# Loading the second x tile from ScalarE's queue in a fused layernorm, attention and gated-MLP kernel

## The chip, the cores and the metric

The kernel runs on one core of a Trainium2 chip. The metric is device time in microseconds (us) of one execution; a value for a kernel is the median over several executions. The profile is one execution recorded by the hardware profiler. Its span, from the first to the last instruction, is a little shorter than the device time of the same execution.

## The reference

All matrices are bf16. x has 2048 rows of 640 values.

```
xn = layernorm(x)                          # over the 640 values of a row
q, k, v = xn @ wqkv                        # 32 heads of 20
logits: each row against rows s, s-2, ..., s-14 (8 of them), masked at the start
o = softmax(logits) * v, summed over the 8
return x + (o reshaped) @ wo + ((xn @ w_gate) * (xn @ w_up)) @ w_down
```

## The kernel before

The rows of x are cut into 16 tiles of 128. A tile is loaded with its rows on the 128 partitions (buffer XST), normalised into XNS, transposed so that its 640 columns lie on the partitions in five chunks (XNT), and multiplied with the weights. The first tiles are transposed by TensorE (L434), later ones by DMA.

The order of work is written out by hand. Every operation is recorded in program order with what it reads and writes; a small scheduler gives each engine its operations in that order, with semaphore waits where data cross engines. So each engine, and each engine's queue of DMA issues, works strictly in the order of the code. Nearly all loads are issued by one helper, so they all carry line 294 in the profile: on SyncE's queue (SPq), or on ScalarE's (ACTq) where the code says so.

The start of the program is what matters here:

- L297 to L307: constants. ScalarE's first instruction is a tiny square root (L324), which brings the load of its function table with it.
- L325: tile 0 is loaded in two halves, one by SyncE and one by ScalarE.
- L328: tile 1 is loaded; L329: the five chunks of the weights of q, called w0 to w4 here (each 128 rows of 640 values, 160 KB as a tile of x is); then tiles 2 and 3, the chunks for k, tiles 4 to 7, and so on.

```
    for half, eng in ((0, "sp"), (1, "act")):
        dst = XST[:, 0, half * DHALF:(half + 1) * DHALF]
        dma(dst, xhbm[0:TS, half * DHALF:(half + 1) * DHALF], w=[dst], name=f"xh{half}", eng=eng)
    x_load(1)
    for c in range(NCH):
        wqkv_load(0, c)
    x_load(2)
    x_load(3)
```

Tile 0's mean and variance are taken by VectorE (L372, L378, L384), its square root by ScalarE (L385), its reciprocal and the normalising by VectorE (L404, L419). Tile 1's sums are taken by ScalarE in the meantime: one pass for the mean (L392), one for the variance (L394), then the square root (L397); VectorE follows with L404 and L419, in two parts of 256 and 384 columns. On ScalarE these three stand behind the square root of tile 0.

TensorE runs matmuls on zeros first (L453), then the five transposes of tile 0 (L434), then the product of tile 0 with w0 to w4, five matmuls of 128 columns for each chunk (L492). Tile 1's five transposes stand between the matmuls with w3 and those with w4; the copies of the transposes out of PSUM are VectorE's (L445) and ScalarE's (L447). Then come tile 1's matmuls (L492), the product for k with two tiles at once (L773), and the rest of the kernel: projections (L499, L475), the gated MLP (L638), its down projection with the attention's output projection (L665, L697). While these run, VectorE does the attention (from L522 on).

Of the kernel before, what the change touches and what calls it, by code (L numbers as in the profile page):

```python
# [211 lines left out]
def build_kernel(nc, A_x, A_wqkv, A_wo, B_x, B_w_gate, B_w_up, B_w_down, out):  # L212
# [80 lines left out]
    def dma(o, i, r=(), w=(), name="", eng="sp", group=None):  # L293
        return op(eng, lambda e: e.dma_start(o, i), r=r, w=w, dma=True, name=name, group=group)  # L294
# [15 lines left out]
    def x_load(t, eng="sp"):  # L310
        dma(XST[:, t % NXS, :], xhbm[t * TS:(t + 1) * TS, :], w=[XST[:, t % NXS, :]], name=f"xld{t}", eng=eng)
# [13 lines left out]
    for half, eng in ((0, "sp"), (1, "act")):  # L325
        dst = XST[:, 0, half * DHALF:(half + 1) * DHALF]
        dma(dst, xhbm[0:TS, half * DHALF:(half + 1) * DHALF], w=[dst], name=f"xh{half}", eng=eng)
    x_load(1)  # L328
    for c in range(NCH):  # L329
        wqkv_load(0, c)  # L330
    x_load(2)
# [622 lines left out]
def bass_parallel_sum__sliding_local_dilated__glu_gated_bilinear__prompt_kernel(  # L954
    nc, A_x, A_wqkv, A_wo, B_x, B_w_gate, B_w_up, B_w_down, out
):
    build_kernel(nc, A_x, A_wqkv, A_wo, B_x, B_w_gate, B_w_up, B_w_down, out)
# [28 lines left out]
```

## Time and profile before

| what | value |
|---|---|
| median of 4 runs | 252.62 us (252.4 to 253.11) |
| profiled execution, device time | 252.48 us |
| its span | 251.1 us |
| TensorE busy | 247.0 us, 98% of the span |
| VectorE busy | 215.7 us, 86% |
| ScalarE busy | 114.0 us, 45% |

Times in the profile count from the start of the span. PE is TensorE, DVE VectorE, ACT ScalarE, SP SyncE; SPq and ACTq are DMA issues on those engines' queues. The duration of an issue is the time that the issuing engine's sequencer takes, not the transfer; the time from issue to landing is given apart. Matmuls are pipelined, so one takes longer (about 0.22 us) than the distance from its start to the next one's. In the table of DMA queues q1 is the row that SyncE's loads run on, q10 the row of ScalarE's.

### The profile page before, as it was taken

Reading aid. Unit: us, or ns where it says so; the run is one execution under the profiler, and the core shown is the slowest. Engines: PE = TensorE matmul, PEld = TensorE weight load, DVE = VectorE, ACT = ScalarE, POOL = GpSimd, SP = SyncE. Lnnn points to the kernel's source line nnn. Section 1 sums busy time; section 2 is a strip of 40 time slices with the busy share of each in tenths; the row PEclk is TensorE's granted clock in tenths of the full one; section 3 lists DMA queues with packets and bytes.
Section 4 is the critical chain, followed back from the end, with each engine's and each line's share of the span. In section 5 each row is a group of like instructions: output and inputs, shape, how many; then the busy total and the mean of one; then the engine's idle time right before and its main releaser. Section 6 shows DMA issues by size and latency. Waiting matters only on the chain.

```text
span 251.1 us, 3245 instructions
## 1 busy us (share of the span) xinstructions
PE 247.0 (98%) x1274; PEld 128.9 (51%) x1294; DVE 215.7 (86%) x255; ACT 114.0 (45%) x203; POOL 32.6 (13%) x41
## 2 busy tenths in 40 slices
PE   8999999999999999999999999999999999999997
PEld 3995555555544444444444444444444444445775
DVE  4879999999999953999999994899999999996212
ACT  5476657555555557555555553225555111011000
POOL 1000001043345231002231100002000000200200
DMA  6999869854787472355369962197500011490561
GB/s 194 300 260 198 106 140 409 235 114 76 146 146 136 87 135 42 130 206 104 64 125 263 402 211 42 39 333 63 90 0 3 21 30 32 67 124 21 81 153 52
DMA packets 33775, 33.78 MB, mean 134 GB/s; under 512 B 17984, under 2 KB 30272, under 8 KB 33728
## 3 DMA queue, kind: packets, MB, share of 16 engines
q1 hardware_dynamic: 27280, 24.13, 35.0%
q0 software_dynamic: 6192, 9.31, 22.7%
q8 instruction: 10, 0.16, 0.3%
q10 hardware_dynamic: 288, 0.13, 0.2%
q14 instruction: 5, 0.04, 0.0%
HBM read 14.42 MB, written 4.59 MB: 76 GB/s over the span
## 4 chain that ended last, share of the span: by engine, by line
PE 96%; DMA 1%; SPq 1%; issue 1%; DVE 0%
PE PS L638 41%; PE PS L665 22%; PE PS L475 21%; PE PS L697 7%; PE PS L499 2%; DMA WQKV<-in_A_wqkv_dram 1%; PE PS L773 1%; PE PS L492 1%; SPq L294 1%; PE PS L434 0%; DVE FOUT L701 0%
## 5 line engine op out<-in xcount | busy, mean ns | idle before, releaser
L638 PE MATMUL PS<-XNT,WU 128*128 128x512 bf16 x237 | 59.0, 379 | 0.2
L638 PE MATMUL PS<-XNT,WG 128*128 128x512 bf16 x232 | 57.9, 379 | 0.4
L475 PE MATMUL PS<-XNT,WQKV 128*128 128x512 bf16 x245 | 53.7, 379 | 0.3
L605 DVE TENSOR_TENSOR PVB<-VO,ATB 128x10240 f16<-128x10240 bf16 x8 | 43.9, 5490 | 0.2
L475 PEld LDWEIGHTS PS<-XNT,WQKV 128*128 128x128 bf16 x250 | 29.4, 118 | 24.4
L640 ACT ACTIVATE USX<-PS 128x512 bf16<-128x512 f32 x48 | 28.7, 597 | 22.6 <-PE PS L638 22.6
L638 PEld LDWEIGHTS PS<-XNT,WU 128*128 128x128 bf16 x240 | 23.5, 98 | 28.3
L638 PEld LDWEIGHTS PS<-XNT,WG 128*128 128x128 bf16 x240 | 23.5, 98 | 28.3
L600 DVE TENSOR_TENSOR PVB<-PVB 128x5120 f16<-128x5120 f16 (+1 forms) x16 | 34.5, 2156 | 0.3
L533 POOL DMA_DIRECT2D LOG<-PE x24 | 21.5, 910 | 59.8 <-DMA LOG<-PE 59.6
L640 ACT ACTIVATE HT<-PS 128x512 bf16<-128x512 f32 x36 | 21.5, 597 | 16.4 <-PE PS L638 16.4
L671 ACT ACTIVATE DT<-PS 128x512 f16<-128x512 f32 x15 | 8.9, 596 | 42.8 <-PE PS L665 39.7
L665 PE MATMUL PS<-HT,WD 128*128 128x512 bf16 x118 | 27.4, 379 | 0.1
L522 DVE TENSOR_TENSOR TMP<-QH,KH 128x2048 f16<-128x2048 bf16 x16 | 19.2, 1218 | 0.5 <-ACT KH L482 0.5
L665 PEld LDWEIGHTS PS<-HT,WD 128*128 128x128 bf16 x120 | 11.8, 98 | 14.1
L522 DVE TENSOR_TENSOR PP<-QH,KH 128x2048 f16<-128x2048 bf16 x16 | 18.9, 1218 | 0.0
L527 DVE TENSOR_TENSOR PP<-PP,TMP 128x4096 f16<-128x4096 f16 x8 | 18.3, 2291 | 0.2
L665 PE MATMUL PS<-VO,WO 128*128 128x512 bf16 x74 | 18.4, 379 | 0.0
L701 DVE TENSOR_TENSOR FOUT<-PS,XR 128x320 bf16<-128x320 f32 (+2 forms) x9 | 4.1, 455 | 15.5 <-PE PS L697 15.5
L533 POOL DMA_DIRECT2D PE<-PP x8 | 8.4, 1045 | 61.5 <-DVE PP L528 61.5
L643 DVE TENSOR_TENSOR HT<-HT,USX 128x512 bf16<-128x512 bf16 x36 | 14.3, 417 | 1.7 <-ACT USX L640 1.7
L482 ACT ACTIVATE VO<-PS 128x512 bf16<-128x512 f32 x20 | 11.8, 593 | 7.2 <-PE PS L475 7.2
(71 smaller groups left out, 220.8 us busy)
## 6 DMA issues: line engine op xcount, KB each, us to landing
PE<-PP POOLq DMA_DIRECT2D x8, 512.0 KB, 5.0
ATB<-LOG SPq DMA_DIRECT2D x8, 512.0 KB, 4.9
LOG<-PE POOLq DMA_DIRECT2D x24, 128.0 KB, 2.7
WG<-in_B_w_gate_dram SPq DMA_DIRECT2D x1, 1920.0 KB, 8.1
WU<-in_B_w_up_dram SPq DMA_DIRECT2D x1, 1920.0 KB, 14.8
WD<-in_B_w_down_dram SPq DMA_DIRECT2D x1, 1920.0 KB, 10.1
out_dram<-in_A_x_dram SPq DMA_DIRECT2D x1, 1920.0 KB, 10.2
out_dram<-FACC POOLq DMA_DIRECT2D x3, 640.0 KB, 6.6
```

What stands on the lines that cost most here:

```text
L475: op("pe", (lambda l, x, c: lambda e: e.matmul(PS[:, b, :], l, x, start=(c == 0), stop=(c == NCH - 1)))(l, x, c), r=[l, x], w=[PS[:, b, :] ...
L482: op("act", lambda e: e.activation(o, PS[:, b, :], ACT.Copy, scale=sc), r=[PS[:, b, :]], w=[o], name=f"pev{which}_{m}_{j}")
L522: return (1.22, lambda: op("dve", lambda e: e.tensor_tensor(o, qw, kw, ALU.mult), r=[q, k], w=[o], name=f"prod{h}_{p}_{c}"))
L527: (2.3, lambda: op("dve", lambda e: e.tensor_tensor(a, a, b, ALU.add), r=[a, b], w=[a], name=f"psum{h}_{p}")),
L533: op("pool", lambda e: e.dma_start(o, i, accum_op=ALU.add), r=[o, i], w=[o], dma=True, name=name)
L600: return lambda: op("dve", lambda e: e.tensor_tensor(o, x, y, ALU.add), r=[x, y], w=[o], name=f"{name}_{b}")
L605: lambda: op("dve", lambda e: e.tensor_tensor(PVB[:], vw, aw, ALU.mult), r=[v, a], w=[PVB[:]], name=f"pv_{b}")),
L638: op("pe", (lambda l, x, c: lambda e: e.matmul(PS[:, b, :], l, x, start=(c == 0), stop=(c == NCH - 1)))(l, x, c), r=[l, x], w=[PS[:, b, :] ...
L640: op("act", lambda e: e.activation(o, PS[:, b, :], ACT.Copy), r=[PS[:, b, :]], w=[o], name=f"guev{which}_{m}_{j}")
L643: h_pending.append(lambda: op("dve", lambda e: e.tensor_tensor(h, h, o, ALU.mult), r=[h, o], w=[h], name=f"h{m}_{j}"))
L665: op("pe", (lambda l, x, i: lambda e: e.matmul(PS[:, b, :], l, x, start=(i == 0), stop=(i == n - 1)))(l, x, i), r=[l, x], w=[PS[:, b, :]], ...
L697: op("pe", (lambda l, x, i, b, wid: lambda e: e.matmul(PS[:, b, 0:wid], l, x, start=(i == 0), stop=(i == n - 1)))(l, x, i, b, wid), r=[l, ...
```

## The change

The load of x tile 1 gets ScalarE's queue in place of SyncE's. On ScalarE it stands behind the tiny square root with its table load and behind ScalarE's half of tile 0. On SyncE the weight chunks follow directly on its half of tile 0. No other operation, buffer or order is touched.

```diff
     for half, eng in ((0, "sp"), (1, "act")):
         dst = XST[:, 0, half * DHALF:(half + 1) * DHALF]
         dma(dst, xhbm[0:TS, half * DHALF:(half + 1) * DHALF], w=[dst], name=f"xh{half}", eng=eng)
-    x_load(1)
+    x_load(1, "act")
     for c in range(NCH):
         wqkv_load(0, c)
     x_load(2)
```

## Prediction, before the change was run

> **What bounds the kernel now.** First the page: the engine row and the chain that ended last.
>
> ```profile
> span 251.1 us, 3245 instructions
> PE 247.0 (98%) x1274; PEld 128.9 (51%) x1294; DVE 215.7 (86%) x255; ACT 114.0 (45%) x203; POOL 32.6 (13%) x41
> PE 96%; DMA 1%; SPq 1%; issue 1%; DVE 0%
> ```
>
> TensorE carries 96% of the chain, so a change in the loads can only matter where the other 4% lie. The chain in order of time (start, duration, what) shows that they lie in the first 7 us:
>
> ```profile
> 2.60 0.44 SPq L294
> 3.08 3.68 DMA WQKV<-in_A_wqkv_dram
> 6.76 0.14 issue
> 6.90 0.45 PE PS L492 x5
> 7.34 0.29 PE PS L434 x5
> ```
>
> SyncE issues its loads one after another, some 0.47 us apart: half of x tile 0, x tile 1, weight chunks w0 to w4. TensorE then waits for w3, issued at 3.08 and landed at 6.76. After 6.90 the chain is TensorE's own until VectorE's last add (0.29 us), with nothing between but issue gaps of 0.05 us, so **a shift of TensorE at about 7.3 us is a shift of the end, one for one**. Read next what surrounds 7.3, in the timeline (start, duration, engine, line):
>
> ```profile
> 0.75 1.28 ACT L324 ACT_TABLE_LOAD   x1 [0.75 <-PEq L971]
> 1.00 0.37 ACTq L294 DMA_DIRECT2D XST<-in_A_x_dram  x1
> ...
> 4.07 0.29 ACT L385 ACTIVATE SD<-MV,EPSC 128x1 f32<-128x1 f32 x1 [1.83 <-DVE MV L384]
> 4.27 0.72 ACT L392 ACTIVATE XNS<-XST 128x640 bf16<-128x640 bf16 x1
> ...
> 6.07 0.29 ACT L397 ACTIVATE SD<-MV,EPSC 128x1 f32<-128x1 f32 x1
> 6.40 0.16 DVE L404 RECIPROCAL SD<-SD 128x1 f32<-128x1 f32 x1 [0.29 <-ACT SD L397]
> 6.60 0.64 DVE L419 TENSOR_SCALAR XNS<-XST,MV,SD 128x256 bf16<-128x256 bf16 x2
> ...
> 7.18 0.45 PE L434 MATMUL PS<-IDENT,XNS 128*128 128x128 bf16 x5
> ```
>
> This is the second chain of tile 1: ScalarE sums it (L392, L394) from 4.27 on, its root comes at 6.07, VectorE normalises it in two parts (ends 6.95 and 7.24), TensorE transposes it from 7.18. Five transposes take 0.28 us or so of the chain, 0.056 each, so the third, the first that needs the second part, is due at about 7.29, some 0.05 us after that part is written. The chain of waits names w3; tile 1's chain is **as late as w3, within 0.05 us**.
>
> Last, how full the transfer engines are. Of the stretches of half a microsecond:
>
> ```profile
> 2.50:3.00 0.50, 0.50 (x2) 0.15 (x1) 0.09 (x1) 0.00 (x0) 0.00 (x0) 1.00 0.98 310
> 3.00:3.50 0.50, 0.50 (x2) 0.15 (x1) 0.50 (x2) 0.00 (x0) 0.00 (x0) 1.00 0.93 292
> ```
>
> The last two columns are DMA share and GB/s. From 2.0 to 6.5 us the share is 0.86 or more. The loads are drained, not issued, at the pace that counts.
>
> **What the Trainium skill says.** "DMA: Bandwidth & Descriptors", section "Issuing engines are not separate DMA queues": loads started by ScalarE and SyncE run on the same 16 engines and interleave; another issuer saves issue time only. Its section "Queues, rings and completion order" says that each DMA engine takes turns between the queues with work, packet by packet. The trace agrees as far as it goes: tile 0's two halves came on two queues and landed 2.1 us after issue each. "ScalarE: Activation LUTs", section "What ACT_TABLE_LOAD costs": 1283 ns; the trace has 1.28. "Perfetto Trace Analysis", section "Sequencer Loop": the sequencer pushes engine work into a queue and goes on. The trace agrees: the load on ACTq started at 1.00, while the table load ran to 2.03.
>
> **The change part by part.**
>
> *SyncE.* One issue (L294) leaves its queue. w0 starts at about 1.19 instead of 1.65, and w1 to w4, x2, x3 and the rest follow 0.46 us earlier. Cost or gain at the transfer engines: nearly none, since the same data (tile 0, tile 1, w0 to w3, six tiles of 160 KB) must still pass before w3 is complete, and the engines have been full since 2.0. At most the tenth that they stand empty from 3.5 to 5.5 us is filled: 0.2 us. And if w3 does land earlier, TensorE does its five matmuls earlier and stops at the transposes of tile 1, whose second part is not written before 7.24. So at most 0.05 us reaches the end. I take 0. The cover is tile 1's chain; without it the gain would be 0.2.
>
> *ScalarE's queue.* It gains one issue, right behind its half of tile 0: start 1.00 + 0.37 + 0.05 = 1.42, against 1.19 on SyncE. Nothing is queued behind it that is due before 4.07, so its 0.4 us costs ScalarE nothing. That the table load holds it up, I exclude for the likeliest case, as the first load was not held up. The two issuers also overlapped (SPq 0.74 to 1.13, ACTq 1.00 to 1.37) without a longer issue on either side.
>
> *Tile 1's transfer.* This is the part with a price. Count packets in the queue table asked from a given time to the end. q1 is SyncE's row, q10 ScalarE's, and a transfer of 128 rows has 144 packets: q10 has 288 for its two (half of tile 0, and a store at the end).
>
> ```profile
> q10 hardware_dynamic: 284, 0.13, 0.2%
> ...
> q10 hardware_dynamic: 144, 0.05, 0.1%
> ...
> q1 hardware_dynamic: 27011, 23.90, 35.0%
> ...
> q1 hardware_dynamic: 26857, 23.73, 34.9%
> ```
>
> From 2.2 on q10 has 284 left, from 2.8 on 144: the half of tile 0 began just before 2.2, 1.2 us after its issue, and was drained by about 2.65 (8 packets were left at 2.6). q1 had 27280 in all; 27011 are left at 3.0 and 26857 at 3.6, which is 154 in 0.6 us or **257 a microsecond** for one queue alone. Tile 1 before (288 packets into q1) was thus drained at about 3.08, and landed at 1.19 + 2.3 = 3.49.
>
> Afterwards tile 1's data can come at 1.42 + 1.2 = 2.62, and begins behind its own queue's half tile at 2.65. From then on w0 and w1 wait in SyncE's queue too, 0.46 us earlier than before, so the two queues take turns: 128 packets a microsecond for tile 1, 144 / 128 = 1.12 us, **drained at 3.78 instead of 3.08**.
>
> From mean drain to landing the slowest engine has to finish. That lag was 0.41 for tile 1, 0.59 for w0 (1.65 + 2.6 = 4.25, drained at about 3.66) and 1.2 for w1 (landed about 5.5, drained at 4.33). Tile 1 now is mixed with just these. Both ends: 0.41 gives 4.19, 1.2 gives 4.98. I take the middle, 0.8: **landing at 4.58**, and 0.04 to start (VectorE's first L372 began at 2.91, its half having landed near 2.85), so 4.62.
>
> *What waits.* L392 was ready at 4.27, after the root of tile 0; x1 had then 0.78 us to spare. Now L392 starts at 4.62: **0.35 late**; from both ends, 0 and 0.75. Behind it on ScalarE stand L394, the root L397 and the copy of tile 1's transposes (L447), all late alike; VectorE's L404 and L419 wait for the root, the transposes for L419, and w4's five matmuls and tile 1's thirty stand behind the transposes on TensorE. The 0.05 us of slack is within the rounding. VectorE's statistics of tiles 2 and 3 come after its copy of tile 1 and shift with TensorE, so no new wait opens there.
>
> *Sum.* 0 for SyncE, 0 for ScalarE's issue, +0.35 for tile 1: the profiled execution, span 251.1 and time 252.48, becomes 252.83. The median of the runs is 252.62, 0.14 above the profiled one; 252.62 + 0.35 is 252.97, say 253.0.
>
> **The rivals.** What a measurement of this kernel can tell from no change is about 0.2%, 0.5 us; the four runs span 0.7.
>
> - *Late by sharing*, the forecast: +0.1 to +0.8. For it: full transfer engines and a chain with 0.05 us of slack. Chance 0.55, about half of it (0.28) above 0.5, which is the side of a landing after 4.73.
> - *Hidden anyway*: tile 1 lands by 4.23, since the first engines to be free favour it or the lag stays at 0.41. Then 0, 252.6. For it: 0.78 us of spare before L392. Against: half the drain rate eats 0.70 of that before any lag. Chance 0.22.
> - *Held up on ScalarE*: the second load of a queue does wait for the table load or for the small ACTIVATE behind it (ends 2.24). Then data from about 3.45, 1.12 to drain, 0.8 lag: 5.4, L392 1.1 late, time 253.7, slower by 0.4%. It decides as soon as the issue starts later than about 1.57, since then the landing passes 4.73. Against: the issue at 1.00 under the table load. Chance 0.14. It is also the case in which the change is "behind the table load" in fact; in the forecast it isn't.
> - *Weights earlier*: w3 lands up to 0.4 us earlier and tile 1 in time. -0.05 for the cap at 7.24; if the cap is softer than I read it, -0.2, 252.4. Beyond -0.5 there is nothing to take: TensorE's whole stop between w2's and w3's matmuls is 6.47 (15 matmuls of 0.056 from 5.64) to 6.90, 0.43. Chance 0.09; 0.03 for faster by over 0.2%, chance of measurement included.
>
> **How the numbers follow.** Slower by over 0.2%: 0.28 + 0.14 = 0.42. Faster: 0.03. Within: 0.27 + 0.22 + 0.06 = 0.55. The time is that of the likeliest, 253.0. The range takes in the landing at its late end and most of the held-up case (253.7 and a little noise), and below the hidden case and half of the last: 252.4 to 253.8.
>
> **What would show it.** Right: on ACTq two issues, the second at about 1.4; SyncE's w0 at about 1.2; tile 1 from issue to landing some 3.2 us instead of 2.3; L392 at about 4.6 with an idle stretch ahead of it put down to DMA XST; the root L397 near 6.4 and the five transposes near 7.5. Wrong: L392 still at 4.27 (hidden); an issue on ACTq after 2.0 (held up); transposes before 7.1 (the cap isn't one); or a shift at 7.5 us that is not found again at the end.

## The result and the profile after

The changed kernel takes 253.01 us (median of 35 runs, 252.58 to 253.65) against 252.54 us for the kernel before in the same comparison (53 runs). The ratio is 1.0018, interval 1.0013 to 1.0023: **slower by 0.47 us**, 0.18%. The forecast was 0.35 us slower. The profiled execution took 252.74 us, its span is 251.4.

The timeline of the kernel after, in the stretch shown for the kernel before (start, duration, engine, line):

```profile
0.74 1.28 ACT L324 ACT_TABLE_LOAD   x1 [0.74 <-PEq L971]
1.00 0.85 ACTq L294 DMA_DIRECT2D XST<-in_A_x_dram  x2
...
1.19 2.31 SPq L294 DMA_DIRECT2D WQKV<-in_A_wqkv_dram  x5
...
4.14 0.29 ACT L385 ACTIVATE SD<-MV,EPSC 128x1 f32<-128x1 f32 x1 [1.91 <-DVE MV L384]
...
4.68 0.74 ACT L392 ACTIVATE XNS<-XST 128x640 bf16<-128x640 bf16 x1 [0.25 <-DMA XST<-in_A_x_dram]
...
6.50 0.29 ACT L397 ACTIVATE SD<-MV,EPSC 128x1 f32<-128x1 f32 x1
...
6.83 0.16 DVE L404 RECIPROCAL SD<-SD 128x1 f32<-128x1 f32 x1 [0.65 <-ACT SD L397]
...
7.03 0.64 DVE L419 TENSOR_SCALAR XNS<-XST,MV,SD 128x256 bf16<-128x256 bf16 x2
...
7.43 0.63 PE L434 MATMUL PS<-IDENT,XNS 128*128 128x128 bf16 x5 [0.17 <-DVE XNS L419]
```

Read it from the top. ScalarE's queue issues twice in a row from 1.00 to 1.85 (the second issue begins at 1.40), under the table load. The weights start at 1.19. ScalarE's sum of tile 1 (L392) starts at 4.68 instead of 4.27, and the bracket now names what ended the idle time before it: the transfer of XST. The root, the normalising and the transposes follow, 0.25 to 0.43 us later than before.

The table of TensorE's waits has changed its entry too. Before it was L492 waiting 0.2 us for w3:

```profile
PE PS L453 <- DVE EPSC L298: 1.0, 1, 1.0
PE PS L434 <- DVE XNS L419: 0.7, 2, 0.6
```

The wait for the weights is gone, and tile 1's transposes wait instead. (0.6 of the 0.7 belong to tile 0's transposes at 5.04, after the matmuls on zeros.) The two events that had met within 0.05 us have come apart: w3 comes a little earlier, and tile 1 later by more than that.

How much of this reaches the end? First the kernel before, then the changed one:

```profile
7.47 1.96 PE L492 MATMUL PS<-XNT,WQKV 128*128 128x128 bf16 x30
9.27 1.36 PE L773 MATMUL PS<-XNT,WQKV 128*128 128x256 bf16 x11
...
7.90 1.84 PE L492 MATMUL PS<-XNT,WQKV 128*128 128x128 bf16 x30
9.57 1.36 PE L773 MATMUL PS<-XNT,WQKV 128*128 128x256 bf16 x11
```

Tile 1's matmuls (L492) start 0.43 later. The product for k (L773) starts 0.30 later: the thirty matmuls took 1.84 us instead of 1.96, which caught up 0.12. From there the two traces run 0.30 apart to the end, which is the difference of the spans. It is less than the 0.47 of the medians, since the profiled execution was one of the quicker ones of the changed kernel (252.74, median 253.01).

One view misleads. The chain that ended last now shows other shares than before:

```profile
PE 92%; SPq 3%; DMA 3%; issue 1%; DVE 1%; ACT 0%
```

Followed in order of time, it leaves TensorE at 18.54 and goes to a load of x issued at 9.30. TensorE didn't stop there: the table of its waits has no such entry, and the gap there is 0.06 us, against 0.05 in the kernel before. An instruction that happened to end just then was taken for the releaser. The table of waits decides.

### The profile page after: what moved, and what is told of

It reads as the page before. It is cut to its first block, busy times and chain, and to the rows that moved or that the text cites. A ratio compares the mean times of both kernels' runs of the same rounds, so it can differ in the third digit from the quotient of the medians.

```text
span 251.4 us, 3245 instructions
## 1 busy us (share of the span) xinstructions
PE 246.7 (98%) x1274; PEld 128.7 (51%) x1294; DVE 216.0 (86%) x255; ACT 114.6 (46%) x203; POOL 32.6 (13%) x41
## 4 chain that ended last, share of the span: by engine, by line
PE 92%; SPq 3%; DMA 3%; issue 1%; DVE 1%; ACT 0%
PE PS L638 41%; PE PS L665 22%; PE PS L475 21%; PE PS L697 7%; SPq L294 3%; DMA XST<-in_A_x_dram 3%; DVE STATS L372 0%; DVE STATS L378 0%; ACT SD L385 0%; DVE FOUT L701 0%; DVE MV L384 0%; DVE SD L404 0%
```

## The experiments

Landings below are the last of a load's 16 engines in the trace. "Over before" is against the kernel before on the same chip. Where an edit adds a line, the profile's line numbers are higher by one or two.

**1. Tile 1 on SyncE's queue, behind w0 or behind w1.**

```diff
-    x_load(1)
     for c in range(NCH):
         wqkv_load(0, c)
+        if c == 0:        # in the second kernel: c == 1
+            x_load(1)
```

> Tile 1 stays on SyncE's queue, but behind w0. It is issued at about 1.65, later than in the changed kernel (1.42). Sharing theory (tile 1 lands late because its packets take turns with the weights'): alone in one queue it is drained behind w0 and lands at 4.2 to 4.3, where w0 landed before; L392 at 4.27 to 4.35; 0 to 0.15 us over the kernel before, about 0.35 faster than the changed one. Rival, the later issue as such costs: another 0.23 us later than in the changed kernel, 0.6 to 0.7 over before.

> Tile 1 on SyncE's queue behind w0 and w1, issued at about 2.12. A dose of lateness without a second queue. Sharing theory, with the end moving one for one: lands where w1 landed before, 5.0 to 5.6, L392 as late, 0.7 to 1.3 us over before. Rival, the start-up has slack that takes most of a delay in: under 0.5 over before.

Behind w0: 252.77 against 252.55, ratio 1.0009 (1.0001 to 1.0017), 0.22 over before. Behind w1: 253.85, ratio 1.0048 (1.0035 to 1.0061), 1.30 over before. Behind w0 the profiled execution had tile 1 landing at 4.69, later than I expected, but the median lies under the changed kernel's although the issue is later (1.65 against 1.40). The rival had 0.6 to 0.7 over before, so the later issue as such isn't the cause. The landing is as late as in the changed kernel, with one queue alone: here w0's packets stand ahead of tile 1's. Behind w1 the landing was 5.83, and ScalarE and TensorE followed it:

```profile
5.85 0.74 ACT L393 ACTIVATE XNS<-XST 128x640 bf16<-128x640 bf16 x1 [1.46 <-DMA XST<-in_A_x_dram]
...
8.60 0.57 PE L435 MATMUL PS<-IDENT,XNS 128*128 128x128 bf16 x4 [1.35 <-DVE XNS L420]
```

In this execution L392 (here L393) starts 1.58 later than in the kernel before, the transposes 1.42 later, and the span is 1.46 longer (252.61 against 251.15). The start-up takes in 0.12 of a delay of 1.58.

**2. A filler in tile 1's old place on SyncE's queue.** To give tile 1 on ScalarE's queue the engines alone for a while, SyncE issues a load that nobody reads before w0.

```diff
     x_load(1, "act")
+    dma(XR[:, 0, 0:16], xhbm[0:TS, 0:16], w=[XR[:, 0, 0:16]], name="fill")
     for c in range(NCH):
```

> The changed kernel, with a load of 4 KB that nobody reads in tile 1's old place on SyncE's queue, so that w0 to w4 go out at their times of before (about 1.65 and on). Only the queue of tile 1 differs from before. Sharing theory: w0's packets come 0.46 later, tile 1 has the engines alone at first and lands at 4.2 to 4.4; L392 at 4.3 to 4.4, 0 to 0.15 us over before. Rival, ScalarE's queue costs by itself (its issue, or a lower share for its row): lands near 4.6 as in the changed kernel, 0.4 to 0.5 over before.

252.99 against 252.55, ratio 1.0016 (1.0009 to 1.0022): 0.44 over before, as the rival had it. The profiled execution, with tile 1 at 4.08, was the fastest of its 21 runs (252.54): it shows what can happen, not what mostly does. The 4 KB filler adds 128 packets ahead of the weights, so I repeated it with one row of 32 bytes, and with two.

> As the run with the filler, but the filler is one row of 32 bytes on one partition, so that it takes SyncE's time and next to nothing of the transfer engines. Sharing theory: tile 1 lands at 4.0 to 4.3, w3 where it did in the kernel before (6.7 to 6.9), 0 to 0.2 us over before; what the filler run had above that came of its 128 small packets ahead of the weights. Rival, ScalarE's queue costs by itself: 0.35 to 0.5 over before again.

> Two such rows ahead of w0, so that w0 goes out 0.9 us later than in the changed kernel and tile 1 has the engines nearly alone. Sharing theory: tile 1 lands at 3.5 to 3.9 from the same issue at 1.42 that brought it to 4.66 beside w0; the end is then w3's, issued 0.47 later than in the kernel before: landing 6.8 to 7.2, 0 to 0.4 us over before. Rival, ScalarE's queue or its issue is what is slow: tile 1 at 4.0 or later.

One row: 253.06 against 252.63, ratio 1.0016 (1.0008 to 1.0025); tile 1 landed at 5.05. Two rows: 252.86, ratio 1.0004 (0.9996 to 1.0012); tile 1 at 4.64. A row takes 0.3 us of issue and not 0.47, so w0 went out at 1.55 and 1.81. Tile 1 missed the expectation in both.

**3. The same without fillers: SyncE waits before w0.** The load of w0 is recorded as reading a constant that GpSimd writes.

```diff
     def wqkv_load(g, c=None, eng="sp"):
         ...
-        dma(dst, wqkv_src[:, cs, g * D:(g + 1) * D], w=[dst], ...)
+        r = [IDENT[:]] if (g, c) == (0, 0) else []     # MSK0 in the second kernel
+        dma(dst, wqkv_src[:, cs, g * D:(g + 1) * D], r=r, w=[dst], ...)
```

> The changed kernel, with SyncE held before w0 by a wait for GpSimd's IDENT (ready at about 1.56) and no filler: w0 goes out at about 1.6, as in the kernel before, and nothing else is added to the transfer engines. Sharing theory: tile 1 has 0.4 us more of the engines alone and lands at 4.0 to 4.3, 0 to 0.2 us over before. Rival, tile 1 on ScalarE's queue is late whenever the weights start (its own packets are slow there, which the filler runs suggest): 4.5 to 5.0, 0.35 to 0.5 over before.

> The same with a wait for GpSimd's MSK0 (ready at about 1.85): w0 at about 1.9. Sharing theory: tile 1 lands at 3.6 to 4.0 and costs nothing; w3, issued 0.25 later than in the kernel before, lands at 6.8 to 7.1 and costs 0 to 0.3 us. Rival, slow in itself: tile 1 at 4.5 or later, 0.35 to 0.6 over before.

Wait for IDENT (w0 issued at 1.59): 253.02 against 252.56, ratio 1.0016 (1.0007 to 1.0024), tile 1 at 5.03. Wait for MSK0 (w0 at 1.88): 252.82, ratio 1.0006 (0.9997 to 1.0014), tile 1 at 4.91. So the landings are the rival's: **with w0 held back by 0.36 to 0.69 us, tile 1 still landed at 4.64 to 5.05 in four of five traces** (4.08 in the fifth). Where w0 was held back by 0.36 to 0.46, no time came back (0.43 to 0.46 over before). Where it was 0.62 and 0.69, about half did (0.23 and 0.26), at the edge of the noise, and that is inside what sharing had for these two. The queue table of the kernel with the wait for IDENT, asked from 2.6 and from 3.2 us to the end, shows that turn-taking can't be what held tile 1 up in that kernel:

```profile
q1 hardware_dynamic: 26992, 23.89, 33.9%
q10 hardware_dynamic: 294, 0.21, 0.4%
...
q1 hardware_dynamic: 26991, 23.88, 34.0%
q10 hardware_dynamic: 242, 0.15, 0.2%
```

In 0.6 us one packet passed on SyncE's row and 52 on ScalarE's, 87 a microsecond. In the kernel before, the same 0.6 us (q1 27120 at 2.6, 26962 at 3.2) passed 158 on one row, 263 a microsecond. The stretches of 0.4 us, with DMA share and GB/s in the last two columns, first of the kernel before:

```profile
2.80:3.20 0.40, 0.40 (x3) 0.12 (x2) 0.29 (x1) 0.00 (x0) 0.00 (x0) 1.00 0.99 314
```

and of the kernel with the wait:

```profile
2.40:2.80 0.40, 0.40 (x3) 0.12 (x2) 0.00 (x0) 0.00 (x0) 0.00 (x0) 1.00 1.10 171
2.80:3.20 0.40, 0.40 (x3) 0.13 (x2) 0.32 (x1) 0.00 (x0) 0.00 (x0) 1.00 0.84 90
```

The engines count as busy (0.84) but move 90 GB/s: each packet takes long. Tile 1 has them to itself and is slow.

Is this ScalarE's queue, and did it slow tile 1 in the changed kernel too? The queue table of a stretch gives the packets that passed in it and the share of the 16 engines' time that they took. Four stretches of 0.6 us: the wait for IDENT from 2.6, the changed kernel from 3.2 (both rows), and SyncE's row in the kernel with the 4 KB filler from 4.4:

```profile
q10 hardware_dynamic: 52, 0.06, 89.5%
...
q10 hardware_dynamic: 98, 0.11, 54.2%
q1 hardware_dynamic: 70, 0.08, 43.6%
...
q1 hardware_dynamic: 47, 0.05, 71.6%
```

Share times 0.6 us times 16, over the packets, is the mean time of one: 165 ns on ScalarE's row in the kernel with the wait, but **53 ns there in the changed kernel, beside 60 on SyncE's**, and 146 on SyncE's row in the last. So slow packets aren't confined to ScalarE's row, and they aren't what made tile 1 drain late in the changed kernel. The kernels that held w0 back had a slow spell of their own just as tile 1 began (85 to 169 ns a packet from 2.6 to 3.2, in all five), which undid what they were built to test. Why it came, these runs don't settle.

**4. ScalarE's loads ahead of the square root.** The square root with its table load moves behind the loads, once in the changed kernel and once in the kernel before (where ScalarE has only tile 0's half).

```diff
-    op("act", lambda e: e.activation(DUM[:, 0:1], EPSC[:, 0:1], ACT.Sqrt), ..., name="sqrt_preload")
     for half, eng in ((0, "sp"), (1, "act")):
         ...
     x_load(1, "act")
+    op("act", lambda e: e.activation(DUM[:, 0:1], EPSC[:, 0:1], ACT.Sqrt), ..., name="sqrt_preload")
```

> The changed kernel, with ScalarE's two loads ahead of the tiny square root. Sharing theory: issues at about 0.74 and 1.15, tile 1 0.2 to 0.27 earlier in the queue, landing at 4.35 to 4.5; 0.1 to 0.3 us over before. Rival, the square root and its table load hold the second load up: taking them away brings tile 1 to 3.6 or earlier and the whole loss goes.

> The kernel before with ScalarE's load of tile 0's half ahead of the tiny square root: the partner of the run in which the changed kernel got this and lost its whole 0.47 us. Sharing theory (there it was tile 1's earlier issue and landing): the kernel before has nothing to gain by it, -0.15 to +0.15 us. Rival, what came back there was tile 0's earlier half or the later table load: the kernel before gains 0.25 us or more as well.

On the changed kernel: 252.56 against 252.55, ratio 1.0001 (0.9993 to 1.0010), the loss is gone. On the kernel before: 252.55 against 252.63, ratio 0.9997 (0.9990 to 1.0003), no difference. The first, in the timeline:

```profile
0.74 0.89 ACTq L294 DMA_DIRECT2D XST<-in_A_x_dram  x2
...
1.67 1.28 ACT L328 ACT_TABLE_LOAD   x1 [1.67 <-PEq L971]
...
4.37 0.72 ACT L392 ACTIVATE XNS<-XST 128x640 bf16<-128x640 bf16 x1
...
7.10 0.63 PE L434 MATMUL PS<-IDENT,XNS 128*128 128x128 bf16 x5
```

Tile 1 landed at 4.33, 0.33 before the changed kernel's 4.66, for an issue 0.22 earlier (1.18). L392 had no idle time ahead of it, and tile 0's root had only ended its turn on ScalarE at about the same time. The time is better than the 0.1 to 0.3 over before that I expected. Had the table load held the second load up, taking it out of the way would have brought tile 1 to 3.6 or earlier; it didn't. This version equals the kernel before and doesn't beat it.

**5. Tile 1's variance pass left out, in both kernels.**

```diff
     ln_sums(1, 0)
-    ln_sums(1, 1)
     ln_sums(1, 2)
```

A second edit, not printed here, has L397 take the root of tile 0's variance instead, so these two kernels leave out a part of the layer norm.

> The changed kernel without tile 1's variance pass (L394): its root is taken of tile 0's variance, so ScalarE's chain of tile 1 is about 0.85 us shorter and nothing else is touched. Sharing theory (the loss is tile 1's chain alone): the chain has slack enough for a landing at 4.6, TensorE waits for w3 as before, and the time is that of the kernel before, -0.15 to +0.1 us. Rival, the loss comes from elsewhere (SyncE's earlier loads colliding with something, or tile 0's second half landing later): 0.3 to 0.5 over before, as in the changed kernel.

> The kernel before without tile 1's variance pass in the same way: the partner of the run on the changed kernel. Both chains meet at 7.2 us; without this one TensorE still waits for w3 at 6.9, so 0 to 0.1 us under before, and the difference to its partner is within 0.15. Rival: if the weights' earlier issue is worth something once tile 1's chain is out of the way, the partner is 0.2 us or more faster than this one.

> The changed kernel on the same chip and in the same rounds as the two others, for a second trace of the landings: 0.35 to 0.6 us over before; tile 1 lands at 4.4 to 4.9 and L392 starts as it lands. Sharing theory: over the traces the end moves with that landing, not with w3's.

On the changed kernel: 252.35 against 252.56, ratio 0.9990 (0.9982 to 0.9998). On the kernel before: 252.57, ratio 1.0001 (0.9993 to 1.0009). The changed kernel again: 253.06, ratio 1.0016 (1.0010 to 1.0023), tile 1 at 4.74. With 0.85 us taken out of tile 1's chain, its landing (4.80 on the changed kernel) costs nothing, and the order of loads that lost 0.47 **gains 0.22** over its partner. That is more than I expected, and what the rival named for the second run. The intervals of the two ratios still touch; the traces have the same 0.20, at the transposes and at the end (spans of 250.9 and 251.1). The transposes of the first, and then of the second (line number one higher):

```profile
6.91 0.44 PE L435 MATMUL PS<-IDENT,XNS 128*128 128x128 bf16 x5
```

```profile
7.11 0.44 PE L435 MATMUL PS<-IDENT,XNS 128*128 128x128 bf16 x5
```

w3 landed at 6.39 in the first and at 6.69 in the second. So the weights' earlier issue is worth about 0.2 us, and the whole loss sits in tile 1's chain.

**The traces together.** In the twelve traces that have the variance pass, TensorE's transposes of tile 1 start at the later of two times: the start of L392 plus 2.74, or the landing of w3 plus 0.42. Both numbers are taken from these traces.

| kernel | tile 1 landed | L392 | w3 landed | the later of the two | transposes began | time of this execution | median over before |
|---|---|---|---|---|---|---|---|
| before | 3.49 | 4.27 | 6.76 | 7.18 (w3) | 7.18 | 252.48 | 0 |
| changed | 4.66 | 4.68 | 6.68 | 7.42 (tile 1) | 7.43 | 252.74 | 0.47 |
| changed, again | 4.74 | 4.76 | 6.38 | 7.50 (tile 1) | 7.51 | 252.82 | 0.50 |
| behind w0 | 4.69 | 4.71 | 6.76 | 7.45 (tile 1) | 7.46 | 252.78 | 0.22 |
| behind w1 | 5.83 | 5.85 | 6.66 | 8.59 (tile 1) | 8.60 | 253.91 | 1.30 |
| filler | 4.08 | 4.10 | 6.85 | 7.27 (w3) | 7.27 | 252.54 | 0.44 |
| filler row | 5.05 | 5.07 | 6.81 | 7.81 (tile 1) | 7.82 | 253.12 | 0.43 |
| two filler rows | 4.64 | 4.66 | 7.15 | 7.57 (w3) | 7.57 | 252.82 | 0.23 |
| wait for IDENT | 5.03 | 5.05 | 6.48 | 7.79 (tile 1) | 7.80 | 253.12 | 0.46 |
| wait for MSK0 | 4.91 | 4.93 | 6.86 | 7.67 (tile 1) | 7.69 | 253.00 | 0.26 |
| changed, issue first | 4.33 | 4.37 | 6.36 | 7.11 (tile 1) | 7.10 | 252.41 | 0.01 |
| before, issue first | 3.80 | 4.37 | 6.84 | 7.26 (w3) | 7.31 | 252.62 | -0.08 |

Eleven of twelve agree within 0.02 us; the last, 0.05 off, is one in which TensorE began tile 0's matmuls late (6.00). The last column is a median over 5 to 35 runs against the kernel before on the same chip; the other columns are one execution each.

The table shows more. In the eight rows in which tile 1 is the later, **the time of the execution is tile 1's landing plus 248.08 us, within 0.01**. And in all fourteen traces, those without the variance pass too, the span ends 241.86 to 241.91 us after the product for k starts: whatever differs between them is settled in the first 11 us. So a time of the changed kernel can be read as a landing. Its median, 253.01, stands for one at about 4.93 (an estimate by this rule), 0.27 later than in the trace shown.

## Why the prediction was right

The side and the mechanism hold: tile 1's load is drained in turns with the weights and lands late, and its chain carries the delay to the end. That the time was met within 0.01 us (253.0 against 253.01) is luck: the start of the sum, four runs with a median of 252.62, lay 0.08 too high, and the shift of 0.35 lay 0.12 too low. Step by step:

- **Tile 1's chain as late as w3, within 0.05 us.** Right. The rule of the two times gives 7.01 for one and 7.18 for the other in the kernel before; the prediction took the second part of the normalising, which ends at 7.24 and is needed by the third transpose. That is the closer reading: the third transpose begins 0.05 us after that part in both traces (7.29 after 7.24, 7.72 after 7.67).
- **SyncE's earlier weights are worth nothing under that cover, and 0.2 without it.** Right both times: w3 landed at 6.68 instead of 6.76 in the changed kernel, and without the variance pass the order gained 0.22.
- **ScalarE's second issue at 1.42, not held up by the table load.** Right: it began at 1.40, the two issues took 0.85 us from 1.00, and the kernel with the table load behind them rules out a wait of the size that was priced.
- **Tile 1 drained at 3.78, by turns.** Right in the mechanism, and nearly in the number. The queue table of the changed kernel, asked from 2.8 and from 3.8 us:

```profile
q1 hardware_dynamic: 26943, 23.82, 34.5%
q10 hardware_dynamic: 324, 0.23, 0.3%
...
q1 hardware_dynamic: 26803, 23.67, 34.5%
q10 hardware_dynamic: 155, 0.06, 0.1%
```

  In this microsecond ScalarE's row passed 169 packets and SyncE's 140, at 50 and 55 ns each on the mean, so the two rows shared the engines and neither was slow. This fits what the Trainium skill's "DMA: Bandwidth & Descriptors" has in "Queues, rings and completion order", that each DMA engine takes turns between the queues with work. (The page's packet is a group of descriptors, while a load of 128 rows counts 144 packets in the trace; the counts show the shares, not the order of the turns.) Two misses nearly cancel in the number. The 324 left at 2.8 are the final store's 144, tile 1's 144 and still 36 of tile 0's half, so tile 1 began after 2.8 and not at 2.65: w0 had slowed that half as well. And tile 1 then passed 133 packets in the microsecond where 128 were forecast; 11 were left at 3.8. What the runs leave open is how early tile 1 would land on ScalarE's queue with no weights beside it, and so what the turns alone cost: the kernels meant to show that had their slow spells.
- **Lag of 0.8 from drain to landing, 4.58.** It was nearly 0.9: 4.66. The last two packets passed only after 4.2 (146 left on ScalarE's row there, 144 at 4.4), so the lag is a tail of a few packets; why they came so late isn't shown. The term was chosen in the middle of 0.41 and 1.2; traces of the same order of loads gave landings at 4.66, 4.74 and 4.80, and the median stands for about 4.93, the late end of the forecast's 4.19 to 4.98.
- **The sum, 0.35.** Measured 0.47. The sum let L392's delay through whole; in the trace 0.41 at L392 became 0.30 at the product for k. By the rule above the forecast's own landing, 4.58, would have given 252.66, only 0.12 over before: the landing was put too early and the passing on too high, and the two made up for each other in part. In detail, L392 started 0.41 late in the profiled execution and 0.49 in the second one. Of the 0.41, 0.17 was w3's share of the stop already and 0.12 was caught up by the thirty matmuls; the chain-bound transposes take 0.63 us instead of 0.45, as they wait again for the second part, which adds 0.18.
- **Not foreseen.** w0's packets also came beside tile 0's second half, which landed at 3.34 instead of 3.08. Tile 0's root moved from 4.07 to 4.14 and TensorE's first matmul from 5.64 to 5.71. Tile 1 was later still, so it cost nothing.

Of the rivals, "hidden anyway" and "held up on ScalarE" fell. The profiled landings (4.66 to 4.80) and L392 at 4.68 answer the first, the issue at 1.40 the second. "Weights earlier" was right on its mechanism and wrong on what ends last.

## What to carry to other kernels

When two chains end within a few hundredths of a microsecond, as here, a gain on one is stopped by the other while a delay on either reaches the end: look for the second chain before you shorten the one that the waits name. A second queue didn't make this load faster; it saved SyncE 0.46 us of issue, gave w3 little, and brought the load on it 1.2 us later, with the weights running beside it. Price a load by its landing, not by its issue, and take the landing from several traces, since it moves by tenths from one execution to the next. And when an experiment removes a cause and the time doesn't come back, look into its trace for a second cause that the edit brought along, before the first is given up.

## What the runs showed of the hardware

- On ScalarE's queue an activation's table load doesn't hold up the loads issued after it: issues at 1.00 and 1.40 lay under a table load from 0.74 to 2.02.
- Loads on SyncE's and on ScalarE's row share the engines: in the changed kernel the two rows passed 70 and 98 packets from 3.2 to 3.8, 60 and 53 ns each. SyncE's row alone passed 158 in 0.6 us of the kernel before.
- Packets can be slow for a spell, on either row, with the engines counted as busy: 165 ns each on ScalarE's row from 2.6 to 3.2 with the wait for IDENT, 146 ns on SyncE's from 4.4 to 5.0 with the 4 KB filler. I had not expected that, and can't explain it.
- A load lands later than most of its packets pass: 0.4 us (tile 1) and 1.2 us (w1) after the mean drain in the kernel before, 0.9 in the changed one, where the last two packets passed after 4.2. The landing, not the drain, is what the next instruction waits for: L392 started 0.02 after it.
